# Windowed attention into a squared-ReLU MLP: copies, a cast and two value tiles at other places in rows 4 to 7

## The chip, the cores and the metric

The kernel runs on one core of a Trainium2 chip. The core has engines that work beside each other: TensorE (PE in the profile) multiplies matrices, VectorE (DVE) and ScalarE (ACT) work element by element, GpSimd (POOL) does casts here and starts some of the transfers, and SyncE (SP) starts the other transfers. Each engine takes its instructions in order, and waits where an instruction needs what another engine has not finished. The metric is the device time of the whole kernel in microseconds (us); less is better. Before the change it is 312.45 us, the median of three runs.

## The reference

There are 8 batches, each with 8 heads, 576 positions and 64 values per head. Heads 0 to 3 look at a sliding window of 32 positions, heads 4 to 7 at every fourth position of a window of 128 (dilated). What attention gives is laid out as 4608 tokens of 512 values, and goes through an MLP with a squared ReLU.

```python
def _attn_ref(q, k, v):
    B, H, S, D = q.shape            # 8, 8, 576, 64
    window, dilation = 32, 4
    scores = (1.0 / np.sqrt(D)) * np.matmul(q, k.transpose(0, 1, 3, 2))
    rel = np.arange(S)[:, None] - np.arange(S)[None, :]
    mask_plain = (rel >= 0) & (rel < window)
    mask_dil = (rel >= 0) & (rel < window * dilation) & (rel % dilation == 0)
    masks = np.stack([mask_plain if h < H // 2 else mask_dil for h in range(H)], axis=0)
    scores = np.where(masks[None], scores, -1000000000.0)
    attn = np.exp(scores - np.max(scores, axis=-1, keepdims=True))
    attn = attn / (np.sum(attn, axis=-1, keepdims=True) + 1e-09)
    return np.matmul(attn, v)

x = attn_out.transpose(0, 2, 1, 3).reshape(B * S, H * D)     # 4608 x 512
r = np.maximum(x @ w_in, 0.0)                                # w_in 512 x 2048
out = (r * r) @ w_out                                        # w_out 2048 x 512
```

## The kernel before

The loop runs over the batches, which the kernel calls rows (b). Beside the attention of row b runs the MLP of one chunk of 512 tokens, chunk b - 1. `pump(n)` issues n small steps of that MLP: so the matmuls of the MLP are put between those of attention, by hand.

```python
    for b in range(2, B):
        pending.append(moe_gen(b - 1))
        nxt = b + 1
        hooks = {}
        if nxt < B:
            after_transposes(b)               # GpSimd waits for row b's transposes (L230)
            ns = load_sliding_qk(nxt)         # GpSimd starts these loads (L112)
            ...
            dd = keep_dilated_qk(nxt)
        if b > 4:
            cast_dilated_v(b)                 # GpSimd (L177)
        kept = []

        def turn():
            kept.append(keep_sliding_qk(nxt, by_token(nxt, ns)))   # VectorE copy (L120), stores
            load_sliding_v(nxt)
            if b > 3:
                cast_sliding_v(nxt)           # GpSimd, 3 casts (L169)

        def turned():
            if nxt < B:
                transpose_sliding(nxt, kept[0])

        def done():
            if nxt < B:
                transpose_dilated(nxt, dd)
                if b > 3:
                    load_dilated_v(nxt, nc.sync)

        if nxt < B:
            hooks[3] = turn
        pump({2: 24, 3: 16}.get(b, 3))
        attn_scores(b, 4 if b == 2 else 3, 0, hooks)
        if b < 4:
            ...
        else:
            attn_values_by_dma(b, (turned, done))
        pump(1000)
```

The scores of a row come in four pairs of PSUM tiles. These, and the tiles of the values, share one pool of two buffers (`pa`). ScalarE takes the exponential of each score tile, VectorE then multiplies by the mask.

```python
    papool = ctx.enter_context(tc.tile_pool(name="papool", bufs=2, space=bass.MemoryType.PSUM))
    pmool = ctx.enter_context(tc.tile_pool(name="pmool", bufs=4, space=bass.MemoryType.PSUM))

    def softmax(u, ps, mask):
        nc.scalar.activation(AT[:, u, 0:UW], ps[:, :, 0 : UW // 2], ACTF.Exp, scale=scale)   # L546
        nc.vector.tensor_mul(AT[:, u, 0:UW], AT[:, u, 0:UW], mask)                           # L547

    def attn_scores(b, gap, less=0, hooks={}):
        for hp in range(2):
            s_sliding(b, hp)          # 12 matmuls into two tiles (L556), then two softmax
            if hp in hooks:
                hooks[hp]()
            pump(gap)
        for g in range(2):
            s_dilated(b, g)           # 16 matmuls into two tiles (L575), then two softmax
            if 2 + g in hooks:
                hooks[2 + g]()
            if g:
                halo_sliding(b, 0)
            pump(gap - less)
```

v lies in blocks of 96 positions, and each block needs the last 32 of the block before. `halo_sliding` copies this overlap on ScalarE (L184), in three parts. The value tiles follow:

```python
    def halo_sliding(b, mp):
        m0, m1 = max(1, 2 * mp), 2 * mp + 2
        nc.scalar.copy(
            vp[b % 2][0:PADP, m0:m1, :, 0:D], vp[b % 2][P - PADP : P, m0 - 1 : m1 - 1, :, 0:D]
        )

    def attn_values_by_dma(b, then):
        xs = x_tiles(b)
        for mp in range(3):
            av_sliding(b, mp, xs)          # 8 matmuls (L605), VectorE normalizes (L588, L593)
            if mp < 2:
                halo_sliding(b, mp + 1)
            else:
                for c in (0, 2):
                    halo_dilated(b, c)     # ScalarE (L189)
            pump(3)
        x_sliding_by_dma(b, xs)
        ys = []
        for t in range(2):
            for a in range(2):
                av_dilated(b, t, a, xs)    # 8 matmuls (L621), VectorE normalizes (L588, L593)
                pump(4)
            if t == 0:
                then[0]()
            ys.append(x_dilated_by_dma(b, t, xs))    # a transpose by DMA (L670)
        then[1]()
        pump(6)
        x_from(b, 0, ys[0])                # ScalarE copy of the transposed tile (L658)
        pump(9)
        x_from(b, 1, ys[1])
```

The MLP's chunk begins with 16 tiles of `x @ w_in` (ph, L293), each with a ReLU on ScalarE (L316) and a square on VectorE (g, L317). Then follows `g @ w_out` by Strassen's scheme, whose products need sums and differences of g's halves. VectorE works them out:

```python
    def sum_of_g(g, f0, f1):
        k = slice(f0 - HF, f1 - HF)
        nc.vector.tensor_add(gs[0][:, k], g[:, k, HTOK:], g[:, f0:f1, HTOK:])      # L326
        nc.vector.tensor_sub(gs[1][:, k], gs[0][:, k], g[:, k, 0:HTOK])            # L327

        # the start of the second product
        nc.vector.tensor_sub(g[:, 0:HF, HTOK:], g[:, 0:HF, 0:HTOK], g[:, 0:HF, HTOK:])   # L401
        yield from product(A, gq(0, 0), wq(0, 0))          # 16 matmuls, pa<-wo,g
        ...
        yield from product(Ck, gq(0, 1), wq(1, 0), (0,))   # 8 matmuls, pc<-wo,g
        yield
        yield from product(A, sq(1), tq(1))                # pa<-wt,gs: needs L327
        ...
        yield from product(Bk, gq(1, 0), tq(2))            # pb<-wt,g: needs L401
        nc.vector.tensor_sub(gs[1], g[:, HF:, 0:HTOK], gs[1])   # L413
```

Of the kernel before, what the change touches and what calls it, by code (L numbers as in the profile page):

```python
# [17 lines left out]
def kernel(  # L18
# [9 lines left out]
    nc = tc.nc  # L28
# [105 lines left out]
    def load_dilated_v(b, eng):  # L134
        vv = v[b, HH:H].rearrange("h (i c) d -> i h (c d)", c=DIL)
        for t in range(2):
            eng.dma_start(out=sd[P - QD[t] : P, t, :, :], in_=vv[Q0D[t] : Q0D[t] + QD[t]])
# [29 lines left out]
    def cast_sliding_v(b, ms=range(0, NB, 2)):  # L167
        for m in ms:
            nc.gpsimd.tensor_copy(  # L169
                vp[b % 2][:, m : m + 2, :, 0:D], sv[:, :, m : m + 2, :].rearrange("p h m d -> p m h d")  # L170
            )

    def cast_dilated_v(b):
        for t in range(2):
            p0 = 64 * t
            for c in range(0, DIL, 2):
                nc.gpsimd.tensor_copy(  # L177
                    vd[b % 2][p0:P, t, c : c + 2, :, 0:D],
                    sd[p0:P, t, :, D * c : D * (c + 2)].rearrange("p h (c d) -> p c h d", d=D),
# [8 lines that stand above are left out]
    def halo_dilated(b, c):  # L188
        nc.scalar.copy(  # L189
            vd[b % 2][0:64, 1, c : c + 2, :, 0:D], vd[b % 2][64:P, 0, c : c + 2, :, 0:D]  # L190
        )
# [34 lines left out]
    seen = const.tile([P, 1], FP16, name="seen")  # L226
# [254 lines left out]
    def moe_gen(c):  # L481
        g = hidden(c)
        yield from mm1_gen(c, g, c > 1)
        yield from (mm2_strassen_gen if c > 1 else mm2_gen)(c, g)
# [10 lines left out]
    def pump(n):  # L495
        for _ in range(n):
            while pending:
                try:
                    next(pending[0])
                    break  # L500
                except StopIteration:
                    pending.pop(0)
# [46 lines left out]
    def s_sliding(b, hp):  # L549
        tiles = [pa(f"ps{b}_{hp}_{half}") for half in range(2)]  # L550
        for half, ps in enumerate(tiles):
            for m3 in range(3):
                m = 3 * half + m3
                for e in range(2):
                    r = slice(D * e, D * (e + 1))
                    nc.tensor.matmul(  # L556
                        ps[:, e, QB * m3 : QB * (m3 + 1)],
                        QKTp[b % 2][r, 1, hp, QB * m : QB * m + P],
                        QKTp[b % 2][r, 0, hp, PADP + QB * m : PADP + QB * (m + 1)],
                        start=True,  # L560
                        stop=True,
                    )
        for half, ps in enumerate(tiles):
            softmax(2 * hp + half, ps, maskp)

    def s_dilated(b, g):
        tiles = [pa(f"pz{b}_{g}_{h}") for h in range(2)]
        for h, ps in enumerate(tiles):
            for a in range(2):
                for t in range(2):  # L570
                    q0 = KPAD + (2 * g + h) * CL + Q0D[t]
                    for e in range(2):
                        r = slice(D * e, D * (e + 1))
                        o = CL * a + Q0D[t]
                        nc.tensor.matmul(  # L575
                            ps[:, e, o : o + QD[t]],
                            QKTd[b % 2][r, 1, a, q0 - PADD[t] : q0 - PADD[t] + P],
                            QKTd[b % 2][r, 0, a, q0 : q0 + QD[t]],
                            start=True,
                            stop=True,  # L580
                        )
        for h, ps in enumerate(tiles):
            softmax(4 + 2 * g + h, ps, maskd)
# [11 lines left out]
    def x_tiles(b):  # L595
        x = xp.tile([QB, 2, NB, 2, D], FP16, name=f"xs{b}", tag="xs")
        return x, [xp.tile([QD[t], DIL, HH, D], FP16, name=f"xd{b}_{t}", tag=f"xd{t}") for t in range(2)]

    def av_sliding(b, mp, xs):
        pav = pa(f"pav{b}_{mp}")  # L600
        for i in range(2):
            m = 2 * mp + i
            for h in range(HH):
                off = (h % 2) * 288 + (m % 3) * QB
                nc.tensor.matmul(  # L605
                    pav[:, i, h * (D + 2) : h * (D + 2) + D + 1],
                    AT[:, 2 * (h // 2) + m // 3, off : off + P],
                    vp[b % 2][:, m, h, 0 : D + 1],
                    start=True,
                    stop=True,  # L610
                )
        normalize(
            b, f"p{mp}", pav, QB, xs[0][:, :, 2 * mp : 2 * mp + 2].rearrange("p c m e d -> p m c e d")
        )

    def av_dilated(b, t, a, xs):
        pav = pa(f"paw{b}_{t}_{a}")
        for e in range(2):
            for h in range(HH):
                off = e * 288 + a * CL + Q0D[t]  # L620
                nc.tensor.matmul(  # L621
                    pav[:, e, h * (D + 2) : h * (D + 2) + D + 1],
                    AT[:, 4 + h, off : off + P],
                    vd[b % 2][:, t, 2 * a + e, h, 0 : D + 1],
                    start=True,
                    stop=True,
                )
        normalize(b, f"d{t}_{a}", pav, QD[t], xs[1][t][:, 2 * a : 2 * a + 2])
# [31 lines left out]
    def x_sliding_by_dma(b, xs):  # L660
        t0 = b * S % XW
        for c in range(2):
            nc.sync.dma_start_transpose(
                out=xT[:, c, t0 : t0 + S].rearrange("x (m q) -> x m q", q=QB),
                in_=xs[0][:, c].rearrange("p m e d -> p (m e d)"),
            )
# [8 lines left out]
    def attn_scores(b, gap, less=0, hooks={}):  # L675
        for hp in range(2):
            s_sliding(b, hp)
# [4 lines that stand above are left out]
            s_dilated(b, g)  # L682
            if 2 + g in hooks:
                hooks[2 + g]()
            if g:
                halo_sliding(b, 0)
            pump(gap - less)

# [25 lines left out]
    def attn_values_by_dma(b, then):  # L714
        xs = x_tiles(b)
        for mp in range(3):
            av_sliding(b, mp, xs)
            if mp < 2:
                halo_sliding(b, mp + 1)
            else:  # L720
                for c in (0, 2):
                    halo_dilated(b, c)
            pump(3)
        x_sliding_by_dma(b, xs)
        ys = []
        for t in range(2):
            for a in range(2):
                av_dilated(b, t, a, xs)
                pump(4)
            if t == 0:  # L730
                then[0]()
            ys.append(x_dilated_by_dma(b, t, xs))
        then[1]()
        pump(6)
        x_from(b, 0, ys[0])
        pump(9)
        x_from(b, 1, ys[1])


    n, m = nsd[0]  # L740
# [64 lines left out]
    n, m = nsd[1]  # L805
# [15 lines left out]
# [5 lines that stand above are left out]
            after_transposes(b)  # L826
            ns = load_sliding_qk(nxt)
            if b == 2:
                cast_v(b)
            dd = keep_dilated_qk(nxt)  # L830
        if b > 4:
            cast_dilated_v(b)
        kept = []

        def turn():
            kept.append(keep_sliding_qk(nxt, by_token(nxt, ns)))
            load_sliding_v(nxt)
            if b > 3:
                cast_sliding_v(nxt)

        def turned():
            if nxt < B:
                transpose_sliding(nxt, kept[0])

        def done():
            if nxt < B:
                transpose_dilated(nxt, dd)
                if b > 3:
                    load_dilated_v(nxt, nc.sync)

        if nxt < B:
            hooks[3] = turn
        pump({2: 24, 3: 16}.get(b, 3))
        attn_scores(b, 4 if b == 2 else 3, 0, hooks)
        if b < 4:
            load_dilated_v(nxt, nc.sync)
            turned()
            done()
            cast_v(nxt)
            attn_values(b, b)  # L860
        else:
            attn_values_by_dma(b, (turned, done))
        pump(1000)
# [33 lines left out]
```

The softmax here doesn't subtract the row's maximum and nothing guards it: scores larger than these inputs give would overflow.

## Time and profile before

| what | us |
|---|---|
| device time, median of 3 runs (lowest, highest) | 312.45 (310.82, 312.85) |
| span of the profiled execution | 309.6 |
| rows b = 4, 5, 6, 7 (from one chunk's first matmul to the next one's) | 31.41, 31.47, 31.43, 30.84 |
| a chunk without attention (253.32 to 279.36) | 26.04 |
| busy in row 6: PE, VectorE, ScalarE, GpSimd | 30.29, 24.73, 20.21, 8.21 |

A line of the profile's timeline gives the start, the busy time, the engine, the line of the kernel, the operation, output and inputs by their names, the shape, and how many instructions of the kind followed each other. In brackets stands how long the engine was idle before it, and what ended the wait. A line of the waits gives who waited for whom, the total in us, how many times, and the longest. The drawn length of a matmul is longer than the time by which it moves TensorE on, since matmuls overlap; the distance of starts shows that time.

### The profile page before, as it was taken

What the parts mean: (1) busy time and instruction counts of PE and PEld (TensorE: products, weight loads), DVE (VectorE), ACT (ScalarE), POOL (GpSimd) and SP (SyncE); (2) the same over time, 40 slices, a digit from 0 to 9 for tenths busy, and PEclk for the clock granted to TensorE, in tenths of its full rate; (3) what the DMA queues carried; (4) which work ended last, traced back from release to release, by engine and by line L of the source; (5) the groups of instructions that cost most, each with busy time, mean ns of one, the idle gap of its engine ahead of it and who ended that gap; (6) DMA issues with size and microseconds to landing.
All of it is one profiled execution on the core that took longest, in us unless ns stands there. A gap on an engine that the chain in (4) does not pass through costs nothing.

```text
span 309.6 us, 6914 instructions
## 1 busy us (share of the span) xinstructions
PE 289.7 (94%) x2762; PEld 192.9 (62%) x2762; DVE 210.8 (68%) x433; ACT 184.7 (60%) x318; POOL 70.4 (23%) x114
## 2 busy tenths in 40 slices
PE   1998998998999999999999999999999999999994
PEld 1554554554455468656788977467745875785583
DVE  7774448567962698489839983999388934834652
ACT  2766648667735883597359734973498346525620
POOL 4472017413705303311242132403030000000000
PEclk9999999999999999999999999999999999999998
DMA  7999997899799969999899979998932131003004
GB/s 119 185 205 212 209 161 122 172 218 218 113 251 208 218 129 185 247 166 205 104 222 219 203 105 205 225 205 108 181 121 40 29 101 46 2 1 139 0 0 138
DMA packets 76752, 45.94 MB, mean 148 GB/s; under 512 B 58352, under 2 KB 69104, under 8 KB 76720
## 3 DMA queue, kind: packets, MB, share of 16 engines
q1 hardware_dynamic: 67648, 30.81, 48.8%
q0 software_dynamic: 9072, 14.68, 27.1%
q8 instruction: 22, 0.36, 0.5%
q14 instruction: 10, 0.08, 0.1%
HBM read 36.70 MB, written 16.52 MB: 172 GB/s over the span
## 4 chain that ended last, share of the span: by engine, by line
PE 56%; DVE 21%; DMA 8%; ACT 7%; issue 3%; SPq 2%; POOL 1%; DVEq 0%; POOLq 0%
PE ph L293 19%; PE pa L370 11%; PE pb L370 8%; PE po L436 7%; DMA ns<-in_q_dram 6%; DVE g L317 5%; DVE xd L593 3%; ACT AT L546 3%; PE pc L370 3%; DVE AT L547 3%; ACT rt L316 3%; DVE xs L593 2%; DVE gs L326 2%; DVE gs L327 2%; PE pf L490 1%
## 5 line engine op out<-in xcount | busy, mean ns | idle before, releaser
L293 PE MATMUL ph<-xT,wi 128*128 128x512 f16 (+1 forms) x640 | 134.0, 359 | 0.7 <-ACT xT L658 0.7
L316 ACT ACTIVATE rt<-ph 128x512 f16<-128x512 f32 x144 | 84.9, 604 | 36.0 <-PE ph L293 35.9
L293 PEld LDWEIGHTS <-wi 128*128 128x128 f16 x640 | 68.3, 114 | 46.0 <-issue 0.6
L317 DVE TENSOR_TENSOR g<-rt 128x512 f16<-128x512 f16 x144 | 63.5, 451 | 38.9 <-ACT rt L316 37.8
L370 PEld LDWEIGHTS <-g 128*128 128x128 f16 x448 | 42.7, 98 | 8.3 <-DVE g L401 2.9
L169 POOL CAST vp<-sv 128x512 f16<-128x512 f32 x24 | 18.8, 815 | 89.9 <-DMA sv<-in_v_dram 76.8
L370 PEld LDWEIGHTS <-gs 128*128 128x128 f16 x336 | 32.2, 98 | 5.5 <-DVE gs L327 1.8
L436 PE MATMUL po<-wo,g 128*128 128x512 f16 x128 | 33.1, 379 | 0.0
L397 DVE TENSOR_TENSOR ov<-pb,ov 128x512 f32<-128x512 f32 x14 | 9.7, 692 | 33.0 <-PE pb L370 17.4
L370 PE MATMUL pb<-wt,g 128*128 128x256 f16 x224 | 27.1, 273 | 1.8 <-DVE g L401 1.8
L370 PE MATMUL pa<-wt,gs 128*128 128x256 f16 x224 | 27.8, 273 | 0.7 <-DVE gs L327 0.7
L386 ACT COPY ov<-pa 128x512 f32<-128x512 f32 x14 | 8.2, 586 | 31.9 <-PE pa L370 31.9
L177 POOL CAST vd<-sd 128x512 f16<-128x512 f32 (+1 forms) x32 | 21.6, 702 | 16.2 <-ACT AT L546 13.4
L547 DVE TENSOR_TENSOR AT<-AT,maskp 128x576 f16<-128x576 f16 x32 | 19.0, 614 | 5.8 <-ACT AT L546 4.8
L593 DVE TENSOR_TENSOR xd<-paw,rcp_d 80x512 f16<-80x512 f32 (+1 forms) x32 | 21.9, 684 | 1.1
L546 ACT ACTIVATE AT<-pz 128x576 f16<-128x576 f32 x32 | 20.0, 707 | 1.7 <-PE pz L575 1.6
L546 ACT ACTIVATE AT<-ps 128x576 f16<-128x576 f32 x32 | 19.2, 660 | 2.4 <-PE ps L556 1.9
L386 ACT COPY ou<-pa 128x512 f32<-128x512 f32 x14 | 8.2, 587 | 16.5 <-PE pa L370 16.5
L593 DVE TENSOR_TENSOR xs<-pav,rcp_p 96x512 f16<-96x512 f32 x24 | 16.5, 687 | 0.8
L547 DVE TENSOR_TENSOR AT<-AT,maskd 128x576 f16<-128x576 f16 x32 | 14.9, 494 | 1.6 <-ACT AT L546 0.7
L621 PEld LDWEIGHTS <-AT 128*128 128x128 f16 x256 | 12.0, 98 | 6.2 <-PE paw L621 1.3
L436 PEld LDWEIGHTS <-g 128*128 128x128 f16 x128 | 10.3, 97 | 8.1
(82 smaller groups left out, 294.2 us busy)
## 6 DMA issues: line engine op xcount, KB each, us to landing
sv<-in_v_dram SPq DMA_DIRECT2D x14, 288.0 KB, 5.6
dp<-nr SPq DMA_DIRECT2D x12, 288.0 KB, 4.1
out_dram<-ou SPq DMA_DIRECT2D x6, 512.0 KB, 4.8
out_dram<-ov SPq DMA_DIRECT2D x6, 512.0 KB, 4.4
sd<-in_v_dram SPq DMA_DIRECT2D x8, 320.0 KB, 5.5
ns<-in_k_dram POOLq DMA_DIRECT2D x8, 288.0 KB, 6.0
ns<-in_q_dram POOLq DMA_DIRECT2D x8, 288.0 KB, 6.8
sd<-in_v_dram SPq DMA_DIRECT2D x8, 256.0 KB, 5.7
```

The source lines that it names most:

```text
L169: nc.gpsimd.tensor_copy(vp[b % 2][:, m : m + 2, :, 0:D], sv[:, :, m : m + 2, :].rearrange("p h m d -> p m h d"))
L177: nc.gpsimd.tensor_copy(vd[b % 2][p0:P, t, c : c + 2, :, 0:D], sd[p0:P, t, :, D * c : D * (c + 2)].rearrange("p h (c d) -> p c h d", d=D),)
L293: nc.tensor.matmul(ph[:, t0:t1], wi4[ffc // 4][:, dmk, :, ffc % 4], xT[:, dmk, x0 : x0 + t1 - t0], start=(dmk == 0 and t0 == 0), stop=(dmk ...
L316: nc.scalar.activation(rt, ph[:], ACTF.Relu)
L317: nc.vector.tensor_mul(g[:, ffc, :], rt, rt)
L370: nc.tensor.matmul(banks[bank][:, t], a(k, t), b(k), start=(new and t == 0 and k == 0), stop=(k == HF - 1), skip_group_check=True,)
L386: nc.scalar.copy(ot, banks[A])
L436: nc.tensor.matmul(po, g[:, ffc, t * P : (t + 1) * P], wo[ffc // 4][:, ffc % 4, :], start=(ffc == 0), stop=(ffc == NFF - 1),)
L546: nc.scalar.activation(AT[:, u, 0:UW], ps[:, :, 0 : UW // 2], ACTF.Exp, scale=scale)
L547: nc.vector.tensor_mul(AT[:, u, 0:UW], AT[:, u, 0:UW], mask)
L593: nc.vector.tensor_tensor(out=x, in0=pv, in1=rb, op=ALU.mult)
L621: nc.tensor.matmul(pav[:, e, h * (D + 2) : h * (D + 2) + D + 1], AT[:, 4 + h, off : off + P], vd[b % 2][:, t, 2 * a + e, h, 0 : D + 1], st ...
```

## The change

It moves work in rows 4 to 7, and takes none away.

- The overlap of sliding v is copied at the row's start (first part) and behind the first and second pair of score tiles (second and third part), rather than between the scores' end and the value tiles, where the first value tile waits for it.
- The two copies of the dilated overlap stand behind the second and third sliding value tile rather than both behind the third.
- The cast of the next row's sliding v, on GpSimd, comes at the chunk's end rather than as soon as v has landed. A one-column copy of the last dilated transpose's result (`seen`) holds it back until that transpose has landed. It is meant to run where VectorE has little to do.
- The third and fourth dilated value tile come two MLP steps later each, so that their normalization stands behind the difference of g's halves (L401) in VectorE's order, and the matmuls that need this difference can begin sooner.

```diff
@@ attn_scores
-            if g:
+            if g and b < 4:
                 halo_sliding(b, 0)
             pump(gap - less)
@@ attn_values_by_dma
             av_sliding(b, mp, xs)
-            if mp < 2:
-                halo_sliding(b, mp + 1)
-            else:
-                for c in (0, 2):
-                    halo_dilated(b, c)
+            if mp:
+                halo_dilated(b, 2 * mp - 2)
             pump(3)
         x_sliding_by_dma(b, xs)
         ys = []
         for t in range(2):
             for a in range(2):
                 av_dilated(b, t, a, xs)
-                pump(4)
+                pump(4 + 2 * (a > t))
             if t == 0:
                 then[0]()
             ys.append(x_dilated_by_dma(b, t, xs))
-        then[1]()
+        then[1](ys[1])
         pump(6)
         x_from(b, 0, ys[0])
-        pump(9)
+        pump(7)
         x_from(b, 1, ys[1])
@@ the loop over rows
         if b > 4:
             cast_dilated_v(b)
+        if b > 3:
+            hooks.update({n: lambda n=n: halo_sliding(b, n + 1) for n in range(2)})
         kept = []
 
         def turn():
             kept.append(keep_sliding_qk(nxt, by_token(nxt, ns)))
             load_sliding_v(nxt)
-            if b > 3:
-                cast_sliding_v(nxt)
...
-        def done():
+        def done(y):
             if nxt < B:
                 transpose_dilated(nxt, dd)
                 if b > 3:
                     load_dilated_v(nxt, nc.sync)
+                    nc.gpsimd.tensor_copy(seen, y[:, 0, 0, 0:1])
+                    cast_sliding_v(nxt)
 
         if nxt < B:
             hooks[3] = turn
+        if b > 3:
+            halo_sliding(b, 0)
         pump({2: 24, 3: 16}.get(b, 3))
```

More of the change, by code (lines that the diff above doesn't have):

```diff
@@ L857 @@
             turned()
-            done()
+            done(None)
             cast_v(nxt)
```

## The prediction

> **What bounds the kernel now.** I looked first at busy time by engine. TensorE leads by far:
>
> ```profile
> PE 289.7 (94%) x2762; PEld 192.9 (62%) x2762; DVE 210.8 (68%) x433; ACT 184.7 (60%) x318; POOL 70.4 (23%) x114
> ```
>
> So only what makes TensorE wait counts. The change touches the rows b = 4 to 7, which in the timeline run from 128.2 to 253.3 us. I therefore asked next for the waits of TensorE in 128 to 254 us (total us, times, longest us):
>
> ```profile
> PE pb L370 <- DVE g L401: 1.8, 4, 0.5
> PE pav L605 <- ACT vp L184: 1.6, 4, 0.4
> PE pa L370 <- DVE gs L327: 0.7, 3, 0.3
> ```
>
> Three waits, once per row each (the last not in row 7), and nothing else. The change names all three. Matmul ends are drawn late in a trace, so I sized the waits from starts. TensorE in row 6, around them (start us, us):
>
> ```profile
> 199.31 0.29 PE L605 MATMUL pav<-vp,AT 128*128 128x65 f16 x4
> 200.00 0.29 PE L605 MATMUL pav<-vp,AT 128*128 128x65 f16 x4 [0.41 <-ACT vp L184]
> ...
> 211.62 0.60 PE L370 MATMUL pa<-wt,gs 128*128 128x256 f16 x4
> 212.48 1.48 PE L370 MATMUL pa<-wt,gs 128*128 128x256 f16 x12 [0.26 <-DVE gs L327]
> 214.44 1.92 PE L370 MATMUL pb<-wt,g 128*128 128x256 f16 x16 [0.48 <-DVE g L401]
> ```
>
> A 256-column matmul advances TensorE by 1.75/16 = 0.109 us (the chain has 16 in 1.75), a 65-column one by 0.032 (8 from 204.53 to 204.78). So the lost times are 200.00 - 199.31 - 4 x 0.032 = 0.56 for the overlap copy, 212.48 - 211.62 - 4 x 0.109 = 0.42 for gs, 214.44 - 212.48 - 12 x 0.109 = 0.65 for g. Rows 4 and 5, read in the same way, give 0.56, 0.41, 0.65 and 0.51, 0.36, 0.65; row 7 gives 0.57, none, 0.49. A second way to the sum: a chunk without attention takes 26.04 us (253.32 to 279.36), row 6's attention matmuls advance TensorE by about 3.7 (4 score pairs of 194.06 - 192.28 - 6 x 0.216 = 0.48, 7 value tiles of 0.255), and row 6 lasts 31.43: 1.7 is idle. The ceiling of the whole change is thus 2.20 (overlap copy) + 1.19 (gs) + 2.44 (g) = 5.83 us, 1.9% of 312.45.
>
> Then the engine behind each wait. VectorE before the two late ones, row 6, and the same two instructions in row 7, where no cast of sliding v runs:
>
> ```profile
> 210.43 0.98 DVE L326 TENSOR_TENSOR gs<-g 128x1024 f16<-128x1024 f16 x1
> 211.45 0.98 DVE L327 TENSOR_TENSOR gs<-gs,g 128x1024 f16<-128x1024 f16 x1
> 212.35 0.19 DVE L588 RECIPROCAL rcp_d<-paw 64x8 f32<-64x8 f32 x1
> 212.57 0.68 DVE L593 TENSOR_TENSOR xd<-paw,rcp_d 64x512 f16<-64x512 f32 x1
> 213.18 1.21 DVE L401 TENSOR_TENSOR g<-g 128x2048 f16<-128x2048 f16 x1
> ...
> 241.85 0.69 DVE L326 TENSOR_TENSOR gs<-g 128x1024 f16<-128x1024 f16 x1
> 242.58 0.69 DVE L327 TENSOR_TENSOR gs<-gs,g 128x1024 f16<-128x1024 f16 x1
> ```
>
> VectorE is never idle from 205.97 to 214.4, so everything ahead of L401 counts. The cast beside it on GpSimd:
>
> ```profile
> 208.85 3.03 POOL L169 CAST vp<-sv 128x512 f16<-128x512 f32 x3 [11.71 <-DMA sv<-in_v_dram]
> ```
>
> And ScalarE in row 6's score stage, which is where the overlap copies go:
>
> ```profile
> 194.66 1.22 ACT L546 ACTIVATE AT<-ps 128x576 f16<-128x576 f32 x2
> 195.72 0.65 ACT L316 ACTIVATE rt<-ph 128x512 f16<-128x512 f32 x1
> 196.19 1.26 ACT L546 ACTIVATE AT<-pz 128x576 f16<-128x576 f32 x2
> 197.26 1.18 ACT L316 ACTIVATE rt<-ph 128x512 f16<-128x512 f32 x2
> 198.22 1.31 ACT L546 ACTIVATE AT<-pz 128x576 f16<-128x576 f32 x2
> 199.55 0.40 ACT L184 COPY vp<-vp 32x256 f16<-32x256 f16 x1
> ```
>
> ScalarE has no gap here: it works without rest from 192.62 to 201.4.
>
> **What the Trainium skill says.** "SBUF — State Buffer", section "Who interferes with whom": a VectorE instruction with two SBUF inputs contends with a GpSimd instruction that reads SBUF. The trace agrees: L326 takes 0.98 us beside the cast and 0.69 without. "ScalarE: Activation LUTs", section "What ACT_TABLE_LOAD costs": an ACTIVATE costs a fixed part plus a time per element, and neighbours overlap by about 0.09 us. The trace agrees roughly: 0.60 for 512 columns alone, and one every 0.49 when queued. "Perfetto Trace Analysis", section "Optimization Strategy": a gap that repeats on the engine that should be saturated can mean too few buffers. No TensorE wait on score buffers shows before; I expect one after (below).
>
> **Part 1, cast of sliding v to the chunk's end.** Three casts in each of rows 4, 5 and 6 start no more when v lands but after the last dilated transpose has landed. That frees L326 and L327: 2 x (0.98 - 0.69) = 0.58 us on VectorE's path, more than the 0.42 that the gs wait costs. At the end of the row GpSimd is idle (in row 6 from 211.9 to the next row), and VectorE has only sums from PSUM left. The casts there take some 1.7 to 3 us (they took 1.72 in row 3, 3.03 in row 6). From about 219 they end by 222, when the next row begins.
>
> **Part 2, dilated tiles 3 and 4 behind L401.** The changed order on VectorE is L326, L327, L401, then both reciprocals and both normalizations. L401 starts 212.57 + 0.68 - 212.35 = 0.9 us earlier, against a wait of 0.65 (0.49 in row 7). On TensorE the fourth tile's 8 matmuls (0.25) now stand between pc and pa<-gs, which adds slack. Together with part 1: L327 ends near 211.8 and L401 near 213.0, where TensorE wants them at 212.3 (the fifth matmul of pa) and 213.6. Both waits go: 1.19 + 2.44 = 3.63 us. The last normalization ends at about 214.7 rather than 215.2, so its transpose isn't delayed in absolute time; measured from the row's shorter end the next row's k and q arrive up to 1 us later.
>
> **Part 3, the overlap copies.** The first (0.40) moves to the row's start, where ScalarE waits 2.0 us for TensorE: free. The second and third (0.60 each) come behind the first and second pair of exponentials, inside the stretch without rest. The score tiles have two buffers, so the next pair of score tiles waits for this pair's exponentials. Walk through row 6: a queued copy adds 0.50 (200.35 to 200.85 in the trace); if it can't overlap the exponential before it, as L184 at 199.55 did not, 0.67. The exponentials of the second pair end at 195.88 before, and 196.4 to 196.55 after; TensorE wants that buffer for pz_0_1 at 196.02: it loses 0.4 to 0.6. Those of the third pair end at 197.45 before, and 198.45 to 198.8 after; with the first delay TensorE wants the buffer at 198.2 to 198.4: another 0.3 to 0.45. Then the first value tile starts 0.7 to 1.05 later than 199.31 but runs through without the 0.56. Balance per row: between -0.13 and -0.5, say -0.3. In four rows the part costs 1.2 us instead of bringing 2.2. The wait for the copy turns into a wait for the score buffers.
>
> **Part 4, the knock-on at VectorE.** Later exponentials make the last masks later (by 1.0 to 1.3 us), and behind them stand L120 and the three value tiles. Between L120 and L326 VectorE has only some 0.5 us to spare. L326 thus starts about 0.5 to 0.7 later, of which TensorE's own delay hides 0.15 to 0.5. Slack left before L327 is about 0.3 us. In rows 5 and 6 the q load that L120 needs (it landed near 200.2, when L120 began) may be late as well. I take 0.2 us off.
>
> **Sum.** 3.63 - 1.2 - 0.2 = 2.2 us; 312.45 - 2.2 = 310.2 us.
>
> **The rivals.** (a) The copies cost nothing: then up to 5.8 us, 306.6. For it speaks that ScalarE is busy only 60%; against it that the score stage has no gap on ScalarE. (b) ScalarE's delay carries on: pending masks, L120 and the value tiles push VectorE so far that the two late waits return in part. Then parts 3 and 4 cost 3 to 4 us and the change comes to nothing, 312 to 313. For it speaks VectorE's small slack, against it 0.58 + 0.9 us gained just there. (c) The cast at the row's end delays GpSimd's next loads of k and q, since they stand behind it in its queue: L120 stalls by a microsecond in rows 5 and 6, 311 to 312. Against it: the loads wait anyway for the dilated transpose (11.1 us of idle before it in row 6). (d) Waits were never worth their length because VectorE's transposes or the loads set the row's length: nothing in TensorE's waits says so.
>
> **Range and chances.** The three runs before spread over 2.0 us (310.82 to 312.85), so 0.6 us either way is noise of a median. (a) and (b) in halves give 307.5 to 312.5; I take 307.8 to 312.6. Faster by over 2% would need more than the whole ceiling of 5.83 us: 0.03. Slower by over 2% would need 6 us of new waits: 0.02. Within 2%: 0.95.
>
> **What would show it.** Part 1: L326 and L327 at 0.69 in rows 4 to 6, GpSimd's casts near the row's end. Part 2: no wait of TensorE for L327 or L401. Part 3: TensorE's wait for L184 gone, new waits of about 0.3 to 0.6 at the score tiles (L575) for exponentials (L546), twice in a row. Part 4: L326 begins no sooner after the row's start than before. Rows of some 30.6 us instead of 31.4. I am wrong if L575 has no wait (then rival a) or L327 and L401 still have theirs (then b).

## The result and the profile after

The changed kernel takes 308.45 us, median of four runs (308.31 to 308.60); beside it the kernel before took 312.01 (310.82 to 312.85). The ratio is 0.989 with a 95% interval of 0.985 to 0.992: faster by 1.1%, where 0.7% was predicted (310.2 us from 312.45) and 307.8 to 312.6 was the range. Measured again on another occasion, it was 0.990 (0.987 to 0.993).

Busy time by engine, the changed kernel:

```profile
PE 288.1 (94%) x2762; PEld 192.3 (63%) x2762; DVE 208.8 (68%) x433; ACT 184.6 (60%) x318; POOL 67.8 (22%) x117
```

TensorE has the same 2762 matmuls and still leads. GpSimd has three instructions more (the holds) and yet 2.6 us less busy time; VectorE has 2.0 us less. Both fit the contention between the two that is shown below. The waits of TensorE, changed kernel, 128 to 254 us (total us, times, longest):

```profile
PE pz L575 <- ACT AT L546: 0.9, 4, 0.2
PE pav L605 <- DVE xs L593: 0.4, 1, 0.4
```

None of the three old waits is left: not the one for L401, not the one for L327, not the one for L184. Two new ones stand there, and both were in the prediction's walk: score tiles (pz) that wait for exponentials, and a value tile that waits because VectorE is late. Row 6 on TensorE (start us, us; what stood idle before in brackets):

```profile
193.52 0.31 PE L575 MATMUL pz<-QKTd 64*128 64x80 f16 x8
194.05 0.31 PE L575 MATMUL pz<-QKTd 64*128 64x80 f16 x8 [0.23 <-ACT AT L546]
194.29 1.48 PE L293 MATMUL ph<-xT,wi 128*128 128x512 f16 x6
195.71 0.71 PE L575 MATMUL pz<-QKTd 64*128 64x80 f16 x16
196.35 1.49 PE L293 MATMUL ph<-xT,wi 128*128 128x512 f16 x6
197.69 0.41 PE L605 MATMUL pav<-vp,AT 128*128 128x65 f16 x8
...
199.50 1.46 PE L293 MATMUL ph<-xT,wi 128*128 128x512 f16 x6
201.37 0.42 PE L605 MATMUL pav<-vp,AT 128*128 128x65 f16 x8 [0.41 <-DVE xs L593]
...
210.01 2.01 PE L370 MATMUL pa<-wt,gs 128*128 128x256 f16 x16
211.86 1.91 PE L370 MATMUL pb<-wt,g 128*128 128x256 f16 x16
```

The same in row 6 of the kernel before:

```profile
195.84 0.43 PE L575 MATMUL pz<-QKTd 64*128 64x80 f16 x16
196.20 1.48 PE L293 MATMUL ph<-xT,wi 128*128 128x512 f16 x6
```

Before, a pair of dilated score tiles advanced TensorE by 196.20 - 195.84 = 0.36 us; now the first dilated pair takes 194.29 - 193.52 = 0.77 and the second 196.35 - 195.71 = 0.64. That is 0.41 + 0.28 = 0.69 lost. The first value tile then runs in one piece. Lower down, pa goes over into pb without a gap: 211.86 - 210.01 = 1.85 for 16 matmuls, against 2.82 before.

VectorE in row 6, the changed kernel:

```profile
199.29 0.76 DVE L120 COPY nr<-ns 128x2304 f16<-128x2304 f16 x1 [0.72 <-DMA ns<-in_q_dram]
...
209.06 0.69 DVE L326 TENSOR_TENSOR gs<-g 128x1024 f16<-128x1024 f16 x1
209.79 0.69 DVE L327 TENSOR_TENSOR gs<-gs,g 128x1024 f16<-128x1024 f16 x1
210.40 1.22 DVE L401 TENSOR_TENSOR g<-g 128x2048 f16<-128x2048 f16 x1
211.53 0.19 DVE L588 RECIPROCAL rcp_d<-paw 64x8 f32<-64x8 f32 x1
```

L326 and L327 take 0.69 as in a row without the cast, and L401 follows at once. L120 now waits 0.72 for the load of q: this is where the late value tile comes from. The cast on GpSimd, changed kernel, row 6:

```profile
216.10 0.19 POOL L847 COPY seen<-yd 128x1 f16<-128x1 f16 x1 [20.80 <-DMA yd<-xd]
216.29 1.72 POOL L169 CAST vp<-sv 128x512 f16<-128x512 f32 x3
```

Alone, the three casts take 1.72 us rather than 3.03. The loads of the next k and q stand behind these casts in GpSimd's order. From row 5 to row 6, changed kernel:

```profile
184.86 1.72 POOL L169 CAST vp<-sv 128x512 f16<-128x512 f32 x3
189.42 0.19 POOL L230 COPY seen<-QKTd 128x1 f16<-128x1 f16 x1 [2.84 <-DMA QKTd<-dd]
190.64 0.64 POOL L112 DMA_DIRECT2D ns<-in_q_dram  x1
```

The casts are done at 186.58, and GpSimd then waits another 2.84 us for the transposes of QKTd before it starts the loads. So the moved cast does not hold them back. ScalarE's score stage in row 6, changed kernel:

```profile
190.29 1.19 ACT L546 ACTIVATE AT<-ps 128x576 f16<-128x576 f32 x2
191.37 0.60 ACT L184 COPY vp<-vp 32x512 f16<-32x512 f16 x1
191.88 1.06 ACT L316 ACTIVATE rt<-ph 128x512 f16<-128x512 f32 x2
192.85 1.15 ACT L546 ACTIVATE AT<-ps 128x576 f16<-128x576 f32 x2
193.91 0.60 ACT L184 COPY vp<-vp 32x512 f16<-32x512 f16 x1
194.41 0.58 ACT L316 ACTIVATE rt<-ph 128x512 f16<-128x512 f32 x1
```

The second pair of exponentials ends at 192.85 + 1.15 = 194.00, and TensorE goes on at 194.05: the buffer wait in one look.

**A measure for the rows alone.** The rows before row 4 are untouched, but their length differs from execution to execution: row 4's first score matmul started between 128.0 and 131.0 us in the profiled executions of all the kernels below. So beside the times I give the stretch from that matmul to the first matmul after row 7 (from the profiled execution alone). Before it is 253.16 - 129.40 = 123.76 us; after, 250.21 - 128.88 = 121.33, or 2.43 less; in the second profile of the changed kernel, 120.67, or 3.09 less. What TensorE loses by starts, set against the 5.83 us of before, gives the stretch within 0.15 us in all kernels below but one, which is named there.

### The profile page after: what moved, and what is told of

It is laid out like the page before. It is cut to its first block, busy times and chain, and to the rows that moved or that the text cites. A ratio compares the mean times of both kernels' runs of the same rounds, so it can differ in the third digit from the quotient of the medians.

```text
span 306.6 us, 6916 instructions
## 1 busy us (share of the span) xinstructions
PE 288.1 (94%) x2762; PEld 192.3 (63%) x2762; DVE 208.8 (68%) x433; ACT 184.6 (60%) x318; POOL 67.8 (22%) x117
## 4 chain that ended last, share of the span: by engine, by line
PE 69%; DMA 9%; ACT 8%; DVE 7%; issue 3%; SPq 2%; POOL 1%; DVEq 0%; POOLq 0%
PE ph L293 27%; PE pa L370 15%; PE pb L370 7%; PE po L436 7%; DMA ns<-in_q_dram 5%; ACT AT L546 4%; PE pc L370 4%; PE paw L621 3%; ACT rt L316 2%; PE pav L605 2%; DMA QKTd<-dd 2%; ACT vp L184 1%; DMA QKTp<-dp 1%; DMA sv<-in_v_dram 1%; DVE xs L593 1%
## 5 line engine op out<-in xcount | busy, mean ns | idle before, releaser
L317 DVE TENSOR_TENSOR g<-rt 128x512 f16<-128x512 f16 x144 | 62.3, 444 | 39.2 <-ACT rt L316 38.4
L169 POOL CAST vp<-sv 128x512 f16<-128x512 f32 x24 | 14.6, 640 | 51.7 <-DMA sv<-in_v_dram 44.7
L546 ACT ACTIVATE AT<-pz 128x576 f16<-128x576 f32 x32 | 19.0, 652 | 1.7 <-PE pz L575 1.6
L546 ACT ACTIVATE AT<-ps 128x576 f16<-128x576 f32 x32 | 18.9, 644 | 1.4 <-PE ps L556 0.8
L547 DVE TENSOR_TENSOR AT<-AT,maskd 128x576 f16<-128x576 f16 x32 | 16.3, 528 | 2.2 <-ACT AT L546 0.7
```

The source lines that it names most:

```text
L169: nc.gpsimd.tensor_copy(vp[b % 2][:, m : m + 2, :, 0:D], sv[:, :, m : m + 2, :].rearrange("p h m d -> p m h d"))
L317: nc.vector.tensor_mul(g[:, ffc, :], rt, rt)
```

## The experiments

My theory: the gain comes from the two waits for VectorE (parts 1 and 2), and the overlap copies (part 3) bring nothing, since one wait takes the place of another. Rivals: the contention with the cast is all of it; or the overlap copies are.

**Part 1 alone**

```diff
             load_sliding_v(nxt)
-            if b > 3:
-                cast_sliding_v(nxt)
...
                     load_dilated_v(nxt, nc.sync)
+                    nc.gpsimd.tensor_copy(seen, y[:, 0, 0, 0:1])
+                    cast_sliding_v(nxt)
```

> The kernel before with part 1 alone (cast of sliding v at the chunk's end). My theory (the gain comes from two waits of TensorE for VectorE): L326 and L327 take 0.69 us in rows 4 to 6, the gs wait goes (1.19 us in three rows), the g wait shrinks only from 0.65 to about 0.49, since TensorE also asks 0.42 sooner: 1.2 + 3 x 0.16 = 1.7 us less, ratio 0.9946. Rival 'the contention with the cast is the whole gain': about 3 us less, ratio 0.990. Rival 'the overlap copies are the gain': no difference, ratio 1.000.

Measured: 309.80 against 311.57 us, ratio 0.9958 (0.9934 to 0.9981), stretch 122.68, that is 1.08 less. TensorE's waits, this kernel, 126 to 253 us:

```profile
PE pav L605 <- ACT vp L184: 1.6, 4, 0.4
PE pb L370 <- DVE g L401: 1.4, 4, 0.5
PE pav L605 <- ACT rt L316: 0.3, 1, 0.3
```

The gs wait is gone, and L326 and L327 take 0.69 in all rows: the removed contention is worth less than the 3 us of its rival. By starts the g wait fell from 2.44 to 2.06 us only, because TensorE reaches it sooner. So the two waits gave 1.19 + 0.38 = 1.57, close to the 1.7 of my theory. The third wait, in row 4, is new and takes 0.42 of that back; it follows a VectorE that waited 1.3 us for q at L120. In row 4 no moved cast has run yet, so this wait is not the cast's doing.

**Part 2 alone**

```diff
                 av_dilated(b, t, a, xs)
-                pump(4)
+                pump(4 + 2 * (a > t))
...
-        pump(9)
+        pump(7)
         x_from(b, 1, ys[1])
```

> The kernel before with part 2 alone (dilated tiles 3 and 4 two MLP steps later). My theory: the g wait goes in all four rows (2.44 us), the gs wait falls by the 0.25 us of the value tile that now stands before it, to about 0.17 in rows 4 to 6; L326 and L327 stay at 0.98: 2.44 + 0.7 = 3.1 us less, ratio 0.990, nearly all of the change. Rival 'contention with the cast': at most 1 us less, ratio 0.997 or more. Rival 'overlap copies': ratio 1.000.

Measured: 309.12 against 311.57 us, ratio 0.9912 (0.9877 to 0.9947), stretch 122.04, 1.72 less.

```profile
PE pav L605 <- ACT vp L184: 1.6, 4, 0.4
PE pa L370 <- DVE gs L327: 1.0, 3, 0.6
```

The g wait is gone in all four rows. The gs wait didn't shrink as expected. TensorE in rows 4 and 6:

```profile
148.26 0.60 PE L370 MATMUL pa<-wt,gs 128*128 128x256 f16 x4
149.12 1.48 PE L370 MATMUL pa<-wt,gs 128*128 128x256 f16 x12 [0.26 <-DVE gs L327]
...
210.01 0.60 PE L370 MATMUL pa<-wt,gs 128*128 128x256 f16 x4
211.20 1.48 PE L370 MATMUL pa<-wt,gs 128*128 128x256 f16 x12 [0.59 <-DVE gs L327]
```

By starts row 4 still loses 149.12 - 148.26 - 4 x 0.109 = 0.42, as before, and row 6 0.75, where L120 had waited 0.73 for q. The 0.25 that I had counted on isn't there: pa<-gs starts 148.26 - 128.92 = 19.34 us after the row's first score matmul, and before the change 148.74 - 129.40 = 19.34 as well. Both value tiles stood ahead of it already. So this part brings the most, but by the stretch less than the 3.1 us that I gave it. The two parts need each other: with the order alone, L327 beside the cast is what ends last.

**Parts 1 and 2, overlap copies where they were**

> The kernel before with parts 1 and 2, the overlap copies where they were. My theory (the copies bring nothing): both waits for VectorE gone, the wait for L184 (0.56 in a row) still there: as the whole change within 0.3 us, ratio 0.988 to 0.990. Rival 'once the others are done, the copies bring their 2.2 us': ratio 0.995.

Measured: 307.40 against 311.64 us, ratio 0.9871 (0.9827 to 0.9916), stretch 121.23, 2.53 less. The whole change has 2.43 to 3.09 less. With the copies left in their place, the kernel is as fast, although L120 waited for q here too (1.3 us in row 4, 1.0 in row 6) and the third value tile lost 0.43 and 0.53 by starts for it.

**Part 3 alone**

> The kernel before with part 3 alone (overlap copies moved as in the change, dilated copies too). My theory: the wait for L184 (2.2 us in four rows) goes, and two waits for exponentials at the score tiles come, about 0.29 each per row: 2.3 us; no difference, ratio 0.999 to 1.002. Rival 'overlap copies': 2.2 us less, ratio 0.993. Rival 'contention': ratio 1.000 as mine, told apart by the trace.

Measured: 311.82 against 311.57 us, ratio 1.0009 (0.9985 to 1.0034), stretch 124.22, 0.46 more.

```profile
PE pb L370 <- DVE g L401: 1.6, 4, 0.5
PE pz L575 <- ACT AT L546: 0.9, 4, 0.2
PE pa L370 <- DVE gs L327: 0.7, 3, 0.3
```

The wait of pav for L184, 1.6 us before, is gone, and that of pz for L546, 0.9, has come. By drawn ends that looks like a gain of 0.7; by starts, 0.69 is lost per row where 0.56 was, and the stretch says the same. This rival has fallen.

**The change without the hold (parts 2 and 3)**

```diff
-                    nc.gpsimd.tensor_copy(seen, y[:, 0, 0, 0:1])
                     cast_sliding_v(nxt)
```

> The changed kernel without the hold: the cast of sliding v starts as soon as v has landed, as before (parts 2 and 3 alone). My theory: L326 and L327 at 0.98 again in rows 4 to 6, TensorE waits for gs 0.2 to 0.6 in each of these rows, the g wait stays away: 1 to 1.5 us more than the changed kernel, ratio to the kernel before 0.992 to 0.994. Rival 'with the tiles behind L401 the place of the cast is indifferent': ratio 0.989.

Measured: 310.09 against 311.64 us, ratio 0.9954 (0.9928 to 0.9980), stretch 122.93, 0.83 less. Without the hold the cast starts as soon as v has landed, inside VectorE's dense stretch again. VectorE and GpSimd, this kernel, row 6:

```profile
209.75 1.06 DVE L326 TENSOR_TENSOR gs<-g 128x1024 f16<-128x1024 f16 x1
210.85 0.98 DVE L327 TENSOR_TENSOR gs<-gs,g 128x1024 f16<-128x1024 f16 x1
211.76 1.62 DVE L401 TENSOR_TENSOR g<-g 128x2048 f16<-128x2048 f16 x1
```

```profile
209.66 2.64 POOL L169 CAST vp<-sv 128x512 f16<-128x512 f32 x3 [12.52 <-DMA sv<-in_v_dram]
```

Now L401, moved forward, falls under the cast too: 1.62 rather than 1.22. By starts TensorE loses 0.42, 0.36 and 0.72 us for gs in rows 4 to 6, and again 0.24 for g in each of them, where I had expected none: 2.2 us in all. The place of the cast isn't indifferent; the one-column copy is worth 1.6 to 2.3 us of the stretch (122.93 against 121.33 and 120.67).

**All overlap copies at the row's start**

```diff
-        if b > 3:
-            hooks.update({n: lambda n=n: halo_sliding(b, n + 1) for n in range(2)})
...
         if b > 3:
-            halo_sliding(b, 0)
+            for n in range(3):
+                halo_sliding(b, n)
         pump({2: 24, 3: 16}.get(b, 3))
```

> The changed kernel with all three overlap copies of a row at the row's start, where ScalarE waits 1.6 us for TensorE. My theory: the waits at the dilated score tiles go in all four rows (4 x 0.57 = 2.3 us), the wait of row 6 for the late load of q may grow by up to 0.5: 1.8 to 2.3 us less than the changed kernel, ratio to the kernel before 0.981 to 0.984. Rival 'ScalarE's total work in the row sets the score stage, not where the copies stand': the waits stay, ratio 0.989.

Measured: 306.28 against 311.57 us, ratio 0.9845 (0.9791 to 0.9898), stretch 119.50, 4.26 less than before. ScalarE, this kernel, start of row 6:

```profile
186.84 0.59 ACT L386 COPY ou<-pa 128x512 f32<-128x512 f32 x1 [1.02 <-PE pa L370]
187.45 1.44 ACT L184 COPY vp<-vp 32x256 f16<-32x256 f16 x3
189.45 0.60 ACT L316 ACTIVATE rt<-ph 128x512 f16<-128x512 f32 x1 [0.56 <-PE ph L293]
```

```profile
PE pav L605 <- DVE xs L593: 1.2, 2, 0.6
```

All three copies fit into 1.44 us in which ScalarE would wait for TensorE, and 0.56 of that time is still left. The waits at the score tiles are gone, and the one for L184 hasn't come back. What is left is the third value tile in rows 5 and 6 (0.77 and 0.71 by starts), behind the late load of q. In a second measurement beside the changed kernel:

> The kernel with all copies at the row's start, beside the changed kernel. My theory: the score waits of four rows (4 x 0.57 = 2.3 us by starts) less what rows 5 and 6 lose at the third value tile beyond the changed kernel: 1.5 us below the changed kernel. Rival 'no difference to the changed kernel' (its intervals of before overlap): under 0.5 us.

> The changed kernel once more, on the same chip as the next two. Ratio to the kernel before 0.989, as the first time.

Measured: 305.93 us (ratio 0.9842, 0.9803 to 0.9882), the changed kernel 307.78 (0.9904, 0.9873 to 0.9934), the kernel before 311.30; stretches 118.66 and 120.67. In this profile the third value tile is late in row 4 alone (0.67). The intervals of the two ratios overlap slightly, but the medians differ by 1.85 us, the stretches by 2.0, and the stretches of the first profiles by 1.8: about 0.6% better than the change.

**L120 behind the second value tile**

```diff
-        if nxt < B:
+        if b < 4:
             hooks[3] = turn
...
             if mp:
                 halo_dilated(b, 2 * mp - 2)
+            if mp == 1:
+                then[2]()          # turn: L120, its stores, the load of sliding v
             pump(3)
```

> The kernel with all copies at the row's start, and L120 (which waits for the load of q) with its stores behind the second value tile rather than behind the scores. My theory: VectorE waits no more for the load in rows 5 and 6, and TensorE no more for the third value tile's buffer (0.55 and 0.60 by the drawn ends, some 0.15 more by starts): 1.2 to 1.5 us less than with the copies at the start, ratio to the kernel before 0.980 to 0.981. Rival 'VectorE is too full in any order': the wait of TensorE turns up at a later tile or at gs, ratio 0.9845 as without it.

Measured: 313.67 against 311.64 us, ratio 1.0052 (1.0027 to 1.0076), stretch 125.86, 6.4 more than with the copies at the start. The aim was reached, L120 doesn't wait any more, and the price was higher. TensorE's only wait in 126 to 253 us, and ScalarE in row 6:

```profile
PE pa L370 <- ACT ov L386: 5.8, 3, 2.2
```

```profile
212.55 0.59 ACT L386 COPY ov<-pa 128x512 f32<-128x512 f32 x1 [2.29 <-PE pa L370]
217.32 1.26 ACT L658 COPY xT<-yd 128x640 f16<-128x640 f16 x1 [4.18 <-DMA yd<-xd]
218.49 0.58 ACT L386 COPY ov<-pa 128x512 f32<-128x512 f32 x1
```

L120's stores and the load of v stand in SyncE's queue ahead of all the row's transposes. They start 11.36 us after row 6's first score matmul (9.55 with the copies at the start), and the transposes into yd 22.23 (20.55), so yd lands later. ScalarE waits 4.18 us for it at L658, and behind L658 stands the copy that frees the bank pa. TensorE waits for that. Both theories had looked at VectorE alone.

The order explains not all of the 6.4 us. By starts these waits are 2.35, 1.58 and 2.40 us in rows 4 to 6, together 6.33, against 1.48 of waits with the copies at the start: 4.85 us. The rest is the clock. In row 6 of this profile (busy times, then the granted clock of TensorE, DMA share, GB/s):

```profile
220.02:223.43 3.41, 3.41 (x19) 2.35 (x17) 0.37 (x1) 1.57 (x5) 0.25 (x1) 0.50 1.11 207
```

At a granted clock of 0.50 a 256-column matmul moved TensorE on by 0.213 us rather than 0.109, so these 3.41 us cost about 1.7. No other profile has such a stretch within rows 4 to 7. The times contain it as well: the mean granted clock is 0.991 over this kernel's 22 runs and 0.999 over the 30 of the kernel before. I estimate from this that up to 0.008 x 310 = 2.5 us of its time come from the clock. Why it fell more often in this kernel was not tried.

**Transposes of QKTd between the two transposes of the value tiles**

```diff
             ys.append(x_dilated_by_dma(b, t, xs))
+            if t == 0:
+                then[2]()          # transpose_dilated(nxt, dd), taken out of done()
```

> The kernel with all copies at the row's start, and the transposes of the next row's dilated q and k (QKTd) put between the two transposes of the dilated value tiles. My theory: GpSimd starts the next loads 2 to 3 us sooner within the row, L120 doesn't wait, the waits of rows 5 and 6 go: 1.2 us less than with the copies at the start, ratio to the kernel before 0.981. Rival 'the second value transpose then lands too late': ScalarE waits longer for yd, and TensorE for ScalarE's copies at the next row's first tiles: ratio 0.985 or more.

> The kernel with the copies at the start and the QKTd transposes between the value tiles' transposes. By its trace, which has 0.2 us of drawn waits left in rows 4 to 7: 1 us below the kernel with the copies at the start, 2.5 us below the changed kernel. Rival (by the first run's median): no gain beyond the copies at the start.

Measured: 306.72 against 311.64 us (0.9851, 0.9820 to 0.9882), and 306.76 against 311.30 (0.9851, 0.9817 to 0.9885); stretches 118.33 and 118.44. The stretch is 1.2 and 0.2 us shorter than with the copies at the start, the whole time isn't. TensorE's wait at the third value tile fell to 0.2 and 0.3 (drawn). In row 6 of the first profile GpSimd started the load of q 1.9 us sooner within the row, but L120, which waited for it, began 9.2 us after this start rather than 7.7, and still waited 0.7. A gain beyond the copies at the start is not shown.

## Why the prediction was right, point by point

| step | predicted | measured |
|---|---|---|
| parts 1 and 2: waits for L327 and L401 | both go, 3.63 us | both gone in both profiles of the change |
| part 3: overlap copies, four rows | 1.2 us lost (0.3 a row; -0.13 to -0.5) | 0.5 lost: 0.69, 0.66, 0.69, 0.69 instead of 0.56, 0.51, 0.56, 0.57 |
| part 4: VectorE late after L120 | 0.2 lost | 0.57 in row 6 of one profile (late load of q), none in the other |
| sum in rows 4 to 7 | 2.2 | 3.63 - 0.53 - 0.57 = 2.53 (stretch 2.43), and 3.10 (stretch 3.09) |

- The waits were read from starts, not from drawn ends, and the sum of such readings meets the stretch within 0.1 us in both profiles. By drawn ends the two VectorE waits were 2.5 us, and part 3 alone would have looked like a gain.
- One reason in part 2 was wrong: that the fourth tile's 8 matmuls, now between pc and pa<-gs, add 0.25 us of slack. They stood ahead of pa<-gs before, too. L327 was early enough all the same, since part 1 had made it 0.58 us earlier against a wait of 0.42.
- Part 3's mechanism was right (the wait for the copy turned into a wait for the score buffers), and its size was at the mild end. The term that was too large is the 0.67 for a copy that can't overlap the exponential before it. In the trace of the change the copy starts at 191.37, before the exponentials end at 191.48. The next ReLU comes at 191.88, after 0.51.
- Part 4's main chain was too dear, and only its second reason came true. Through the later masks L326 was to start 0.5 to 0.7 us later in the row. Where L120 did not wait for q, L326 started only 0.13 to 0.26 later (18.14 to 18.17 us after the row's first score matmul before, 18.29 to 18.40 after), of which 0.13 is TensorE's own delay, and TensorE did not wait for it.
- What it cost came from the load of q. In the profiles of all kernels the third value tile was late by more than 0.1 us only in rows in which L120 had waited 0.57 us or more. The load lands at another time in each execution: in row 6 of one profile of the change L120 waited 0.72 and began 8.65 us after the load's start, in the other it began 7.99 after it and did not wait. What decides it was not settled.
- That the 2.43 us of the first profile come so near to the 2.2 predicted is in part luck: part 3 cost 0.67 less than predicted, and the late load 0.37 more. In the second profile, without the late load, it is 3.09.
- Rival (a), that the copies cost nothing, is refuted for the place where the change puts them, and true for the row's start: there, rows 4 to 7 come to 4.26 and 5.10 us less. With all three waits gone one expects 5.83, less what the third value tile still loses. Rival (b) didn't come. Rival (c) didn't come either: the load is late in some rows, but GpSimd waits 1.8 to 2.8 us for the transposes of QKTd after the moved cast in both profiles of the change, and L120 waits as well where no moved cast stands before the load (0.73 in row 6 of part 2 alone, 1.3 in row 4 of part 1 alone).
- The medians differ by 3.56 us, and the rows by 2.4 to 3.1. In the two profiled executions the spans differ by 3.0: 2.43 in rows 4 to 7, 0.52 ahead of row 4 and 0.05 behind row 7, both of which the change doesn't touch. The part ahead of row 4 varies by 3 us between executions; where the rest of the medians' difference lies is not traced.

## What to carry to other kernels

An engine in order that is busy 60% of the whole may be full in the very stage that counts: move a small copy to where the engine waits by itself (here ScalarE at the row's start), not merely ahead of its reader. When two waits stand one behind the other, remove both: with the first one gone (part 1 alone), 2.06 of the second one's 2.44 us were left, since TensorE reached it sooner. And before an instruction is put off, follow its queue as well as its engine: what stands behind it in a transfer queue is put off too, and its readers with it.

## What the runs showed of the hardware that was not expected

- Contention between VectorE and GpSimd goes both ways. Sums and differences of two SBUF tensors on VectorE took 0.98 to 1.06 rather than 0.69 us (128x1024) and 1.62 rather than 1.22 (128x2048) beside GpSimd's casts; the three casts took 2.64 to 3.59 us beside VectorE's work and 1.72 alone.
- The same pair of exponentials on ScalarE became longer where no copy stood in between: 1.19, 1.22, 1.26, 1.31 us for the four pairs of row 6 before, and 1.19, 1.15, 1.15, 1.16 in the changed kernel. That the second wait at the score tiles is smaller than the first fits this. With the copies at the row's start the four are 1.19, 1.22, 1.26, 1.31 again. The cause was not tried.
